# Query features of six tiles turned through memory instead of by TensorE

## The chip, the cores and the metric

The kernel runs on one core of one Trainium2 chip. The metric is the device time of one execution in microseconds (us). The engines are called PE (TensorE), DVE (VectorE), ACT (ScalarE), POOL (GpSimd) and SP (SyncE, which here only issues DMAs).

## The reference

Two branches work on one normalised input and are added to it:

```python
xn = layernorm(x)                                   # S=2048 rows, D=512
# branch A: linear attention, 32 heads of 16, features by two softmaxes
q, k, v = split(xn @ wqkv)
phi_q = concat(softmax(q @ w_phi), softmax(-q @ w_phi))
phi_k = concat(softmax(k @ w_phi), softmax(-k @ w_phi))
kv, z = phi_k^T v, sum(phi_k)
A = (phi_q kv / (phi_q z + 1e-6)) @ wo
# branch B: gated MLP with a product over the rows
z1, z2 = split(gelu(xn @ w_in)); z2 = layernorm(z2)
B = (z1 * (w_sp @ z2 + b_sp)) @ w_out
return x + A + B
```

## The kernel before

Rows are worked in 16 tiles of 128 (`NT`). Large products split each float operand into a rounded part and a remainder and do three matmuls (`mm3`, lines 56 to 58). Up to about 490 us the kernel computes the projections, the softmax features and the product with `w_sp`; what matters here is the last stage, which joins both branches.

At its start, the query features of tile `s` (unnormalised exponentials and reciprocal sums) lie in the DRAM tile `e_d`, and the gated values of branch B, already with features as rows, in `u_d`. The last stage walks over pairs of tiles `i`, `i + 1`. On PE a pair is:

1. `attend_T(i)`, called at the end of the pair before: the features of both tiles (128 rows by 1024 features each) are transposed into PSUM, 16 transposes of 128x128 (line 936, line 934 for the pair of tiles 2 and 3), and ACT copies them to four tiles `f` (features as rows, 256 columns). `f` has five buffers.
2. `project_u(i)`: 17 matmuls of `u` with `w_out` (`pout`).
3. `attend`: 16 small matmuls of the stationary `kvT` with `f` (`po`, line 951), which ACT and DVE split into `oT`.
4. `project_u(i + 1)`.
5. `project_o(i)` and `project_o(i + 1)`: 12 matmuls each of `oT` with `wo` into the same `pout`. ACT copies the sum out, and POOL adds it to `out` by an accumulating DMA.

Ahead of that run the preparations. `load_q` (line 535, SP) loads the features `et` of a tile from `e_d`, five tiles ahead. `features(s)` (three tiles ahead) calls `q_fin` (lines 542 to 549, DVE), which divides them by the attention's denominator in place, using a scratch tile `qtmp`; then a DMA issued by POOL (line 905) copies the result to a tile `er` of another number kind, of which there are six. `fetch_u` (lines 813 and 814, SP) loads `u` and its rest `rt` four tiles ahead; `gated` splits `u` into `uh` (ACT) and `ul` (DVE). The gated values of tiles 14 and 15 are made late, inside pair 8: DVE turns them in 32x32 blocks into `zt` (line 795, STREAM_TRANSPOSE), and SP stores them to `u_d` in four DMAs (line 798), with runs of 128 bytes.

`et` and `qtmp` share one pool of 16 slots (`slot`) with other tiles of this stage. The order on each engine is set by a planner that simulates the program while it is built: it takes what is ready, by the order of the program, and so lets preparations run ahead on an idle engine. `issue_after(ins)` keeps the instructions of its block behind `ins`, but only those on the engine of `ins`. The queues of the engines are then worked in that fixed order; an instruction that waits holds up what stands behind it on its engine, and this holds for the DMAs that SP issues.

Of the kernel before, what the change touches and what calls it, by code (L numbers as in the profile page):

```python
# [10 lines left out]
F32 = mybir.dt.float32  # L11
# [7 lines left out]
P = 128  # L19
# [4 lines left out]
NG = 4  # L24
NF = 2 * D
# [3 lines left out]
BL = 32  # L29
EPS_LN = 1e-5  # L30
EPS_DEN = 1e-6
XB = 5
FT, LT = 6, 13
NP = NT // 2
HP, QP = P // 2, P // 4
FP = 3 * P
# [4 lines left out]
def mixer(ctx: ExitStack, tc: tile.TileContext, x, x_t, wv, wqkT, phi_bd, wo, w_in, wst, b_r, w_out, out):  # L41
    nc = tc.nc
    pe, act, dve, pool, sp = nc.tensor, nc.scalar, nc.vector, nc.gpsimd, nc.sync
# [27 lines left out]
    def xz_tile(n, dt, name):  # L71
        return xz.tile([P, SL], dt, tag="xz", name=name)[:, :n]

    mid = ctx.enter_context(ExitStack())
    dram = ctx.enter_context(tc.tile_pool(name="dram", bufs=1, space=DRAM))
# [2 lines left out]
    u_d = dram.tile([NT, FU, P], F32, name="u_d")  # L78
    kvT_d = dram.tile([P, D], F32, name="kvT_d")
    zb_d = dram.tile([P, NF], F32, name="zb_d")  # L80
    nm_d = dram.tile([NT, ND, P], F32, name="nm_d")

    ident = cst.tile([P, P], F32, name="ident")
# [13 lines left out]
    def heads(ap):  # L97
        return ap.rearrange("p (h d) -> p h d", d=DH)

    def group(e, j):  # L100

        return e[:, j * P:(j + 1) * P]

    def pairs(ap, a):
        return ap.rearrange("p (h a) -> p h a", a=2)[:, :, a]

    def bc(ap, n):
        return ap.unsqueeze(2).to_broadcast([P, n, DH])
# [25 lines left out]
    def zproj(ps, s, w, order=(0, 1)):  # L134

        if ps in (za, kv_ps_p):
            p = [ps.tile([P, D], F32, tag="z", name="zps") for _ in range(2)]
        else:
            q = ps.tile([P, 2, D], F32, tag="z", name="zps")
            p = [q[:, k] for k in range(2)]  # L140
        t = xT[s]
        for k, j in enumerate(order):
            for c in range(ND):
                cs = slice(c * P, (c + 1) * P)
                zproj.last = mm3(p[k][:, :FC], (t[:, 0, cs], t[:, 1, cs]), (w[j][0][:, c], w[j][1][:, c]), c == 0, c == ND - 1)
        return [(slice(k, k + 1), p[k][:, :FC].unsqueeze(1)) for k in range(2)] if ps in (za, kv_ps_p) else [(slice(0, 2), q[:, :, :FC])]
# [28 lines left out]
    with ExitStack() as p0:  # L175
        res = p0.enter_context(left("p0res", 1))
        wk = p0.enter_context(left("p0wk", 2))
# [234 lines left out]
        t = xz_tile(2 * D, F32R, "xT").rearrange("p (a b) -> p a b", a=2)  # L412
# [18 lines left out]
        p = ps.tile([P, D], F32, tag="mm", name="proj")  # L431
# [7 lines left out]
        p = ps.tile([P, D], F32, tag="mm", name="proj")  # L439
# [18 lines left out]
        p = ps.tile([P, D], F32, tag="mm", name="proj")  # L458
# [79 lines left out]
    def q_fin(et, tmp, zb):  # L538

        e, r, t, w = et[:, :NF], *(et[:, NF + k * 2 * H:NF + (k + 1) * 2 * H] for k in range(3))  # L540
        den = et[:, NF + 6 * H:QW]
        dve.tensor_tensor(tmp, e, zb, op=ALU.mult)
        dve.tensor_reduce(t, heads(tmp), axis=AX.X, op=ALU.add)
        dve.tensor_tensor(t, t, r, op=ALU.mult)
        dve.scalar_tensor_tensor(den, pairs(t, 0), EPS_DEN, pairs(t, 1), op0=ALU.add, op1=ALU.add)
        dve.reciprocal(den, den)
        dve.tensor_tensor(w.rearrange("p (h a) -> p h a", a=2), r.rearrange("p (h a) -> p h a", a=2),
                          den.unsqueeze(2).to_broadcast([P, H, 2]), op=ALU.mult)
        return e, dve.tensor_tensor(heads(e), heads(e), bc(w, 2 * H), op=ALU.mult).ins

    QC = 4
    NQ = NT // QC
    NC = NP * NQ


    SEQ = [(i, q) for i in range(NP) for q in (range(NQ) if i < NP - 1 else (1, 2, 3, 0))]

# [5 lines left out]
    def load_a(n):  # L563
        i, q = SEQ[n]
        f = []
        for k in range(2):
            t = ws.tile([P, QC, P], F32, tag=f"f{k}", bufs=2, name="wf")
            sp.dma_start(t, wst[2 * i + k, :, q * QC:(q + 1) * QC, :])
            f.append(t.rearrange("p (k two) t -> p two k t", two=2))
        return f  # L570

    def prep_a(n, f):

        a, b = f
        pl = hl[n % 2]
        ops = {}

        def parts(names, src):
            t = pl.tile([P, 2, len(names), 2, P], F32R, tag="".join(names), name="A")
            prep_a.last = b_parts(t[:, 0], t[:, 1], src)  # L580
            for k, m in enumerate(names):
                ops[m] = t[:, 0, k], t[:, 1, k]

        sums = (sm[0].tile([P, 4, 2, P], F32, name="S") if sm else
                zw.tile([P, 4, FC], F32, tag=("T", "z2")[n], bufs=n + 1, name="S").rearrange("p a b -> p (a b)")[:, :8 * P].rearrange("p (a k b) -> p a k b", a=4, k=2))
        parts(("A11", "A12"), a)
        dve.tensor_tensor(sums[:, 0], b[:, 0], b[:, 1], op=ALU.add)
        dve.tensor_tensor(sums[:, 1], sums[:, 0], a[:, 0], op=ALU.subtract)  # L588
        parts(("S1", "S2"), sums[:, 0:2])
        dve.tensor_tensor(sums[:, 2], a[:, 0], b[:, 0], op=ALU.subtract)  # L590
        dve.tensor_tensor(sums[:, 3], a[:, 1], sums[:, 1], op=ALU.subtract)
        parts(("S3", "S4"), sums[:, 2:4])
        parts(("A22",), b[:, 1:2])
        return ops
# [3 lines left out]
    with ExitStack() as p1:  # L598
        tmp1 = p1.enter_context(left("tmp1", 1))
        kvT = tmp1.tile([P, D], F32, name="kvT")  # L600
        zb = tmp1.tile([P, NF], F32, name="zb")
# [41 lines left out]
        for s in range(NE):  # L643
            et = load_q(s, tb.tile([P, QW], F32, name="et") if s else tmp1.tile([P, 4, D], F32, tag="zhl", name="et").rearrange("p a b -> p (a b)")[:, :QW])
            tmp = zw.tile([P, 4, FC], F32, tag="z2", bufs=2, name="qtmp").rearrange("p a b -> p (a b)")[:, :NF]
            e, _ = q_fin(et, tmp, zb)
# [57 lines left out]
    for s in range(NT):  # L704
        p = zproj((kv_ps_p, zc, zbp, za)[s % 4], s, w2, (0, 1) if s % 2 == 0 else (1, 0))
# [7 lines left out]
        for k, q in p:  # L713
            ins = act.activation(z[:, k], q, AF.Gelu_apprx_tanh, scale=r_x[:, s:s + 1]).ins
# [35 lines left out]
    def load_z1(i):  # L750
        t = gt.tile([P, 2, FH + REM], F32, tag="z1", name="z1t")
        for k in range(2):
            pool.dma_start(t[:, k, :FH], z1_d[2 * i + k])  # L753
        return t

    def products(n, g):
        i, q = SEQ[n]
        ops = A.pop(n)
        for name, an, bn in FORM:
            if n % NQ == 0:  # L760
                g[name] = psg.tile([P, D], F32, tag="g", name="g")
            dst = g[name][:, :FC]
            for k in range(2):
                (ah, al), (bh, bl) = ops[an], B[2 * q + k][bn]
                mm3(dst, (ah[:, k], al[:, k]), (bh, bl), n % NQ == 0 and k == 0, n % NQ == NQ - 1 and k == 1)
# [16 lines left out]
    def gate(i, cb, z, u, ut, after=None):  # L782
# [10 lines left out]
        def turn():  # L793
# [3 lines left out]
            for b in range(0, P, BL):  # L797
                (pool if i == NP - 2 else sp).dma_start(dst[:, :, b:b + BL], src[b:b + BL].rearrange("p (m b) -> p m b", b=BL))

        return turn  # L800

    def slot(name, dt=F32):
        return xz_tile(2 * FH, dt, name)
# [44 lines left out]
    g, es, ets = {}, {}, {}  # L848
    for n in range(NC):
        i = SEQ[n][0]  # L850
        if n % NQ == 1 and i < NP - 1:
            z = load_z1(i)
        products(n, g)
        if n % NQ == NQ - 1 and i < NP - 1:
            c = gt.tile([P, 2, FU], F32, tag="c", name="c")
            cq = c[:, :, :FH].rearrange("p k (j f) -> p k j f", j=2)
            cb = drain(i, g, cq)
            g = {}
        if n + 3 < NC:
            raw[n + 3] = load_a(n + 3)  # L860
        if n + 2 < NC:
            A[n + 2] = prep_a(n + 2, raw.pop(n + 2))
        if n % NQ == NQ - 1 and i < NP - 1:
            turn = gate(i, cb, z, c, z, prep_a.last)
# [4 lines left out]
        if n == NC - 3:  # L869
            zs = slot("zb", F32R)  # L870
            zb, ident_r = zs[:, :NF].bitcast(F32), zs[:, NF:NF + P]
# [5 lines left out]
        if n == NC - 2:  # L877
            es[0], es[1] = first_q(0), first_q(1)
            t = xz_tile((KF + 1) * P, F32R, "u1")
# [10 lines left out]
    wk = ctx.enter_context(left("cwk", 2))  # L890
# [5 lines left out]

    def features(s):
        with tc.issue_after(fin[-1]):
            es[s], ins = q_fin(ets.pop(s), slot("qtmp")[:, :NF], zb)
        fin.append(ins)  # L900
        if s == 3:
            return
        e = es[s]
        es[s] = cw.tile([P, NF], F32R, tag="er", bufs=6, name="er")
        lasts[6] = pool.dma_start(es[s].bitcast(F32), e).ins
# [19 lines left out]
    def attend_T(s):  # L925

        fs = []
        for g in range(NG):
            pt = pst.tile([P, 2, 2, P], F32, tag="tr", name="ptq")
            for a in range(2):  # L930
                for k in range(2):
                    src = group(es[s + k], 2 * g + a)
                    if src.dtype == F32:
                        pe.transpose(pt[:, a, k], src, ident)
                    else:
                        pe.transpose(pt[:, a, k].bitcast(F32R), src, ident_r)  # L936
            f = wk.tile([P, 2, 2 * P], F32, tag="f", bufs=NG + 1, name="f")
            lasts[5] = act.activation(f, pt.rearrange("p a k b -> p a (k b)"), AF.Copy).ins
            fs.append(f)
        return fs  # L940
# [50 lines left out]
    GATE_LAST = 8  # L991

    fT = attend_T(0)
    wk.tile([P, D], F32, tag="xr", bufs=3, name="xr")
    wk.tile([P, 10 * QP], F32, tag="gap", name="gap")
# [20 lines left out]
    p, nxt = {}, dict(enumerate(uT))  # L1016
# [61 lines left out]
```

## Time and profile before

| | us |
|---|---|
| median of 3 runs | 625.21 (624.02 to 629.76) |
| the profiled execution | 625.34 |
| its span, first to last instruction | 623.6 |
| busy in the span: PE, DVE, ACT, POOL | 615.1, 508.3, 272.8, 113.7 |
| mean granted clock of PE | 0.999 |

Times in the rows of the profile count from the start of the span. A row of a timeline gives the start, the duration, the engine, the line and what it does; several alike in sequence are merged and counted with x. In brackets stands the idle time before it and what ended it. Matmuls overlap, so the distance between two starts says more than a duration.

### The profile page before, as it was taken

To read this page: it belongs to the slowest core of one execution; us is meant where nothing else is said; L and a number is where in the kernel's file an instruction comes from. 1 tells how busy PE (TensorE), PEld (TensorE's weight loads), DVE (VectorE), ACT (ScalarE), POOL (GpSimd) and SP (SyncE) were. 2 spreads that over 40 slices of the span, in tenths; PEclk is the share of its full clock that TensorE was granted. 3 is DMA by queue.
4 is the path that set the end of the run, shared out by engine and by line. 5 is a ranking of instruction groups with operands and counts; after the bars stand their busy time and mean duration, and the time that the engine had idled before them with its cause. 6 is when DMAs were issued, how large, how long until landed. Compare 5 with 4: busy or idle time off the path is not lost.

```text
span 623.6 us, 11439 instructions
## 1 busy us (share of the span) xinstructions
PE 615.1 (99%) x4366; PEld 561.5 (90%) x4366; DVE 508.3 (82%) x903; ACT 272.8 (44%) x436; POOL 113.7 (18%) x198
## 2 busy tenths in 40 slices
PE   8999999999999999999999999999999999999997
PEld 7888888878889999999999999999999887788785
DVE  5999899899988498988989888696959899989211
ACT  4652324333433558876435433253444433334331
POOL 4122233222211025541000000000000212211110
PEclk9999999999999999999999999999999999999999
DMA  9557676566546757002464745637477799984722
GB/s 318 189 138 165 162 183 187 152 165 172 118 154 186 271 210 270 2 1 67 129 128 136 196 89 155 156 97 173 88 177 244 225 284 332 328 243 111 162 38 48
DMA packets 90671, 103.67 MB, mean 166 GB/s; under 512 B 47080, under 2 KB 60136, under 8 KB 90376
## 3 DMA queue, kind: packets, MB, share of 16 engines
q1 hardware_dynamic: 76840, 60.76, 34.0%
q0 software_dynamic: 11472, 36.54, 23.6%
q10 hardware_dynamic: 2304, 5.64, 2.4%
q8 instruction: 34, 0.56, 0.4%
q14 instruction: 21, 0.17, 0.1%
HBM read 61.61 MB, written 30.56 MB: 148 GB/s over the span
## 4 chain that ended last, share of the span: by engine, by line
PE 85%; DMA 6%; DVE 4%; issue 3%; POOL 1%; ACT 1%; DVEq 0%; POOLq 0%
PE g L58 11%; PE g L57 10%; PE g L56 10%; PE zps L58 6%; PE zps L56 6%; PE zps L57 6%; PE pout L56 5%; PE pout L58 5%; PE pout L57 5%; DMA xc<-nm_d 5%; PE proj L56 4%; PE proj L57 4%; PE proj L58 4%; PE ptq L936 1%; PE po L951 1%
## 5 line engine op out<-in xcount | busy, mean ns | idle before, releaser
L57 PE MATMUL g<-B,A 128*128 128x344 f32 x448 | 143.4, 320 | 0.0
L56 PE MATMUL g<-B,A 128*128 128x344 f32 x448 | 142.9, 320 | 0.0
L58 PE MATMUL g<-B,A 128*128 128x344 f32 x448 | 140.7, 321 | 0.1
L56 PEld LDWEIGHTS g<-B,A 128*128 128x128 f32 x448 | 84.3, 188 | 0.0
L57 PEld LDWEIGHTS g<-B,A 128*128 128x128 f32 x448 | 84.2, 188 | 0.0
L58 PEld LDWEIGHTS g<-B,A 128*128 128x128 f32 x448 | 83.7, 188 | 0.4 <-DVE A L52 0.4
L48 ACT ACTIVATE A<-S 128x512 fp32r<-128x512 f32 x64 | 39.2, 629 | 76.3 <-DVE S L588 61.3
L121 ACT ACTIVATE e<-e,r_x 128x1024 f32<-128x1024 f32 x26 | 29.9, 1150 | 56.3 <-DVE e L120 55.1
L56 PE MATMUL proj<-wqk_h,xT 128*128 128x512 f32 x128 | 50.1, 391 | 0.0
L57 PE MATMUL proj<-wqk_l,xT 128*128 128x512 f32 x128 | 50.0, 390 | 0.0
L58 PE MATMUL proj<-wqk_h,xT 128*128 128x512 f32 x128 | 49.9, 390 | 0.0
L48 ACT ACTIVATE A<-wf 128x512 fp32r<-128x512 f32 (+1 forms) x64 | 33.1, 519 | 33.3 <-DMA wf<-in_wst 12.6
L52 DVE TENSOR_TENSOR A<-S,A 128x512 fp32r<-128x512 f32 x64 | 43.0, 686 | 4.4 <-ACT A L48 4.0
L56 PE MATMUL zps<-w_0h,xT 128*128 128x344 f32 x128 | 41.1, 321 | 0.0
L56 PE MATMUL zps<-w_1h,xT 128*128 128x344 f32 x128 | 40.9, 319 | 0.0
L58 PE MATMUL zps<-w_0h,xT 128*128 128x344 f32 x128 | 40.8, 319 | 0.0
L58 PE MATMUL zps<-w_1h,xT 128*128 128x344 f32 x128 | 40.7, 319 | 0.0
L57 PE MATMUL zps<-w_1l,xT 128*128 128x344 f32 x128 | 40.6, 318 | 0.0
L57 PE MATMUL zps<-w_0l,xT 128*128 128x344 f32 x128 | 40.6, 318 | 0.0
L753 POOL DMA_DIRECT2D z1t<-z_d x16 | 8.6, 545 | 166.9 <-DMA u_d<-z1t 124.9
L52 DVE TENSOR_TENSOR A<-wf,A 128x512 fp32r<-128x512 f32 (+1 forms) x64 | 35.0, 549 | 1.8 <-ACT A L48 1.8
L124 DVE TENSOR_REDUCE sm<-e 128x64 f32<-128x1024 f32 x26 | 31.2, 1200 | 1.7 <-ACT e L121 1.5
(218 smaller groups left out, 1430.6 us busy)
## 6 DMA issues: line engine op xcount, KB each, us to landing
wf<-in_wst SPq DMA_DIRECT2D x64, 256.0 KB, 3.1
e_d<-e POOLq DMA_DIRECT2D x16, 544.0 KB, 5.0
et<-e_d SPq DMA_DIRECT2D x16, 544.0 KB, 5.2
er<-et POOLq DMA_DIRECT2D x12, 512.0 KB, 5.5
z_d<-z1f ACTq DMA_DIRECT2D x16, 344.0 KB, 2.3
z1t<-z_d POOLq DMA_DIRECT2D x16, 344.0 KB, 5.3
zacc<-e POOLq DMA_DIRECT2D x10, 512.0 KB, 4.7
u<-u_d SPq DMA_DIRECT2D x15, 320.0 KB, 6.3
```

Of the source, the lines that this page charges most:

```text
L48: return act.activation(h, src, AF.Copy).ins
L52: return (eng or dve).tensor_tensor(l, src, h.bitcast(F32), op=ALU.subtract).ins
L56: pe.matmul(dst, ah, bh, start=start, stop=False)
L57: pe.matmul(dst, ah, bl, start=False, stop=False)
L58: return pe.matmul(dst, al, bh, start=False, stop=stop).ins
L121: softmax_pair.last = less, act.activation(e, e, AF.Exp, scale=scale).ins
L124: dve.tensor_reduce(sm, heads(e), axis=AX.X, op=ALU.add)
L753: pool.dma_start(t[:, k, :FH], z1_d[2 * i + k])
L936: pe.transpose(pt[:, a, k].bitcast(F32R), src, ident_r)
L951: lasts[3] = pe.matmul(po[r][c * QP:(c + 1) * QP, k], kvT[rows, m // 2, cols], fs[m // 4][rows, m // 2 % 2], start=True, stop=True).ins
```

## The change

For tiles 10 to 15 (`TQ = 10`), the features are not copied to `er`. DVE turns them in 32x32 blocks into `qtmp` (one instruction on 128x1024), and SP stores them in four DMAs to a new DRAM tile `q_d`, which holds the features of a pair as rows and its 256 positions as columns. Each DMA takes 32 partitions and writes runs of 32 floats, 128 bytes. `attend_T` of these three pairs then makes no transposes and no ACT copies: it loads each of the four `f` tiles (256 KB, rows of 1 KB) from `q_d` by SP. Pairs 0 to 8 stay as they are.

```diff
+TQ = 10
+    q_d = dram.tile([NP, NF, 2, P], F32, name="q_d")
+    def turn_q(s, dst, e):
+        ins = dve.transpose(dst, e).ins
+        q = q_d[s // 2, :, s % 2].rearrange("(m j) t -> j m t", j=BL)
+        for b in range(0, P, BL):
+            turn_q.last = sp.dma_start(q[:, :, b:b + BL], dst[b:b + BL].rearrange("p (m t) -> p m t", t=BL)).ins
+        return ins
+
+    def load_f(s, f, g):
+        sp.dma_start(f, q_d[s // 2, 2 * g * P:2 * (g + 1) * P].rearrange("(a p) k t -> p a (k t)", p=P))
+        return f
@@ def features(s):
         with tc.issue_after(fin[-1]):
-            es[s], ins = q_fin(ets.pop(s), slot("qtmp")[:, :NF], zb)
+            tmp = slot("qtmp")[:, :NF]
+            es[s], ins = q_fin(ets.pop(s), tmp, zb)
+            if s >= TQ:
+                ins = turn_q(s, tmp, es.pop(s))
         fin.append(ins)
+        if s >= TQ:
+            return
@@ def attend_T(s):
         fs = []
+        if s >= TQ:
+            return [load_f(s, wk.tile([P, 2, 2 * P], F32, tag="f", bufs=NG + 1, name="f"), g) for g in range(NG)]
```

## The prediction

> **What bounds the kernel now.** I read the page first, its busy times and the chain that ended last, then the last 127 us, where the edit lies, stage by stage, and then the timelines of the engines there.
>
> ```profile
> PE 615.1 (99%) x4366; PEld 561.5 (90%) x4366; DVE 508.3 (82%) x903; ACT 272.8 (44%) x436; POOL 113.7 (18%) x198
> ...
> PE 85%; DMA 6%; DVE 4%; issue 3%; POOL 1%; ACT 1%; DVEq 0%; POOLq 0%
> ```
> ```profile
> 497.00:540.00 43.00, 43.00 (x288) 34.37 (x272) 40.51 (x64) 15.18 (x27) 9.43 (x14) 1.00 1.03 314
> 540.00:580.00 40.00, 40.00 (x280) 31.56 (x280) 36.02 (x56) 16.51 (x29) 7.76 (x12) 1.00 0.73 195
> 580.00:610.00 30.00, 30.00 (x205) 23.82 (x205) 3.77 (x5) 10.23 (x19) 3.41 (x4) 1.00 0.48 96
> ```
>
> The columns of the stages are: length, then busy time of PE, weight loads, DVE, ACT and POOL, the granted clock, the DMA share and GB/s. PE is busy in every microsecond from 497 to 610 at full clock, and the chain is PE's. DVE is nearly full up to 580 (36.02 of 40) and almost empty after that. The DMA engines are full up to 540 and have room later. So what counts in the tail is PE's string of work; the other engines count only if they make it wait. In order of time, the chain shows that string for the pairs of tiles that the edit touches (10/11, 12/13, 14/15):
>
> ```profile
> 571.16 1.34 PE ptq L936 x16
> ...
> 576.46 1.02 PE po L951 x32
> 577.48 0.43 PE pout L56
> ...
> 587.07 1.31 PE ptq L936 x16
> ...
> 592.36 1.02 PE po L951 x32
> ...
> 602.97 1.34 PE ptq L936 x16
> ...
> 608.27 1.02 PE po L951 x32
> ```
>
> A pair costs 15.9 us (576.46 to 592.36): 16 transposes of query features (L936), the first tile's `w_out` product, the attention (`po`), the second tile's `w_out` product, two `wo` products. No wait of another engine stands between them. The attention comes about 5.3 us after the transposes began; that is the time in which ScalarE now copies `f` out of PSUM.
>
> **The change part by part.** *Removed from PE:* 16 transposes in each of three pairs.
>
> ```profile
> 570.76 0.39 PE L58 MATMUL pout<-woh,oT 128*128 128x512 f32 x1
> 571.00 1.50 PE L936 MATMUL ptq<-zb,er 128*128 128x128 f32 x16
> 572.33 0.46 PE L56 MATMUL pout<-wu,uh 128*128 128x512 f32 x1
> 572.63 0.39 PE L57 MATMUL pout<-wu,uh 128*128 128x512 f32 x1
> ```
>
> From the last `wo` matmul to the second `w_out` matmul there are 572.63 - 570.76 = 1.87 us. Without the transposes two pitches would be left; one pitch is 571.00 - 570.76 = 0.24 (0.23 elsewhere), so 0.46. That saves 1.41 us a pair. By the chain's own pieces it is 1.34, 1.31 and 1.34, so the sum lies between **3.99 and 3 x 1.41 = 4.23 us**. I take 4.2, since the slow first matmul after the transposes goes as well. Is something else late next? The first `w_out` product behind the freed place needs the split `u` of tile 10, and the second one the output buffer that ScalarE empties:
>
> ```profile
> 560.66 0.83 DVE L52 TENSOR_TENSOR ul<-u,uh 128x640 fp32r<-128x640 f32 x1 [1.83 <-ACT uh L48]
> ```
> ```profile
> 571.24 0.60 ACT L983 ACTIVATE xr<-pout 128x512 f32<-128x512 f32 x1 [1.04 <-PE pout L58]
> ```
>
> The split is done by 561.5, ten microseconds before 571.2, and the buffer is empty by 571.8 and used again at 577.5. So nothing is.
>
> The transposes have another price in the groups, that of each by itself:
>
> ```profile
> L936 PE MATMUL ptq<-zb,er 128*128 128x128 f32 x96 | 8.9, 247 | 0.0
> ```
>
> Each lasts 247 ns, but the 96 of six pairs fill 8.9 us, 93 ns each: they overlap, and their places in the row are what counts. The Trainium skill, in "TensorE: Matmul & The Clock Gate", Part 4: PE-mode transpose, measured about 275 ns for one inside a kernel; 48 of those would be an estimated 13.2 us where I take 4.2. The durations agree with it and the pitch does not.
>
> *Removed elsewhere:* 12 ScalarE copies of `f` (4 a pair) and six `er<-et` copies issued by POOL. ScalarE and POOL are idle most of this stretch (16.51 and 7.76 of 40), so this gives nothing by itself; it frees DMA time.
>
> *Added to DVE:* six transposes of 128x1024. The one of 128x1472 is the nearest row:
>
> ```profile
> 548.95 1.22 DVE L549 TENSOR_TENSOR et<-et 128x1024 f32<-128x1024 f32 x1
> ...
> 561.66 1.22 DVE L549 TENSOR_TENSOR et<-et 128x1024 f32<-128x1024 f32 x1
> ...
> 569.55 1.22 DVE L549 TENSOR_TENSOR et<-et 128x1024 f32<-128x1024 f32 x1
> ...
> 571.82 1.71 DVE L795 STREAM_TRANSPOSE zt<-z1t 128x1472 f32<-128x1472 f32 x1
> ...
> 577.32 1.22 DVE L549 TENSOR_TENSOR et<-et 128x1024 f32<-128x1024 f32 x1
> 578.45 1.28 DVE L52 TENSOR_TENSOR oT<-po,oT 128x512 fp32r<-128x512 f32 x2
> ```
> ```profile
> 581.42 0.40 PE L56 MATMUL pout<-woh,oT 128*128 128x512 f32 x1
> ```
>
> 1.71 x 1024/1472 = 1.19 us each, 7.1 us in all (at most 6 x 1.71 = 10.3). The L549 rows end the features of tiles 11, 13, 14 and 15 (550.2, 562.9, 570.8, 578.5). DVE has 4.0 us idle between 540 and 580, so the last features come some 3 us later (between 2 with all idle time used and 6 with none). That lies beside PE: before, tile 15's features were ready 25 us ahead of their use at 603. What PE does wait for on DVE are the `oT` remainders, queued among the features: here they end at 579.7, and the `wo` products begin at 581.42. A transpose put ahead of them costs at most 1.2 us, inside that 1.7. I price it at 0; with the cover gone it is 1.2 a pair.
>
> *Added to SP:* 24 stores of 128 KB in pieces of 128 bytes, and 12 loads of 256 KB.
>
> ```profile
> 552.54 0.55 SPq L535 DMA_DIRECT2D et<-e_d  x1
> 573.55 5.84 SPq L798 DMA_DIRECT2D u_d<-zt  x4
> 584.66 0.38 SPq L813 DMA_DIRECT2D u<-u_d  x1
> ...
> 586.17 0.47 SPq L814 DMA_DIRECT2D rt<-u_d  x1
> ```
> ```profile
> SPq L798 <- DVE zt L795: 20.4, 1, 20.4
> ...
> SPq L813 <- DMA u_d<-zt: 5.1, 2, 3.4
> ```
> ```profile
> q1 hardware_dynamic: 7488, 1.51, 26.5%
> ...
> wf<-in_wst SPq DMA_DIRECT2D x64, 256.0 KB, 3.1
> ...
> u<-u_d SPq DMA_DIRECT2D x15, 320.0 KB, 6.3
> ...
> u_d<-zt SPq DMA_DIRECT2D x4, 184.0 KB, 4.6
> ```
>
> The stores of `zt` are of the same kind: four in 5.84 us of SP. By size, a tile's four take 5.84 x 128/184 = 4.1 us of SP and land 4.6 us later. The queue row is from the DMA view of 570 to 600: 26.5% of 16 engines over 30 us is 127 engine-us for 7488 packets, 17 ns each. So a tile's 4096 pieces occupy all 16 engines for 4.4 us, 26 us in all six, and the share of 0.73 and 0.48 in the two stages leaves 10.8 + 15.6 = 26 us; the loads of `f` take the place of the six `er` copies, which move the same bytes. It fits, without anything to spare. The Trainium skill ("DMA: Bandwidth & Descriptors", Specifications) sets 512 bytes as the least size for the full rate, which speaks against this store. The trace agrees: 128 bytes in 17 ns on 16 engines is 120 GB/s, where the full stretch moved 314.
>
> A load is priced at 0.4 us of SP, landing after 3.1 (`wf`) to 6.3 us (`u`); I take the upper, as the DMA engines are busy.
>
> *Added waits.* The stores wait for DVE's transpose; behind them in SP's order stand the loads of later tiles and the `zt` stores. SP issued nothing from 553 to 573.5, so this is free. The loads of `f` wait for the stores and for the attention of the pair before, which holds four of the five `f` buffers; behind them stand tile 14's and 15's `u`, the last `x` and the last stores. The attention waits for `f`; behind it stands all of PE. `qtmp` is held until the stores land, about 10 us, but the last `et` load was issued at 552.5 for features that end at 578.5 and take about 6 us, so a late slot has cover.
>
> When is `f` due? At 576.46 - 1.41 = 575.0, 592.36 - 2.82 = 589.5 and 608.27 - 4.23 = 604.0. When is it there?
> - Pair 10: features 11 end at about 552 with a transpose of lag, turned by 553, stored by 557 and landed by 562; buffers are free at 561.5. Loads issued by 564 land by 570: 5 us early.
> - Pair 12: buffers are free at 577.48 - 1.41 = 576.1; features 13 landed by 576. If the loads go out then, they land by 584. If they stand behind tile 14's stores and `zt`'s (575 to 579, then to 584.4), they are issued by 586 and land between 589.1 and 592.3: a wait of 0 to 2.8 us.
> - Pair 14: features 15 are turned by 582.7, stored by 587, landed by 591.4; buffers are free at 590.6. Loads land by 600: 4 us early.
>
> **Sum:** 625.34 us for the profiled execution (span 623.6) less 4.2 is 621.1. The median shown is 625.21, which is the same within 0.02%, so **621.1** stands for both.
>
> **The rivals.**
> 1. *Pair 12's loads stand behind the `zt` stores.* For it: both become ready at about 576 on one queue. Against it: the loads may go first, and the shorter landing just fits. Late DVE remainders end in the same place. Price 1 to 4 us in all: 622 to 625, say 623.2.
> 2. *Slower: pair 12's loads stand behind the `u` loads of tiles 14 and 15.* Those wait on SP until the `zt` stores have landed (the 5.1 us in SP's waits). With the lag that is 584.4 + 4.6 = 589.0; the `u` and `rt` loads take to 590.9, `f` is issued by 592.5 and lands between 595.6 and 598.8. PE waits 6 to 9 us and gives back more than it got: 621.1 + 6 to 9 = **627 to 630**, say 628. It decides from the point where `f` lands more than 4.2 us after 589.5. Against it: the `u` loads become ready 8 us later than the `f` loads. Over 1% slower needs a wait of 10.5 us.
> 3. *Each transpose is worth its whole duration to PE:* 48 x 0.247 = 11.9 us, so 613.5. The two pitches around 16 of them, 1.87 us, speak plainly against it. The Trainium skill's 275 ns stands for this case.
> 4. *The change doesn't do what it says:* PE finds another wait in the freed place and the time stays at 625. The two rows on the split `u` and the output buffer speak against it.
>
> **How the numbers follow.** Forecast (no notable wait) 0.57; rival 1 0.22; rival 2 0.12; rival 3 0.02; rival 4 0.07. One per cent, 6.3 us, is about what a measurement here can tell from no change. All but rival 3 and the far end of rival 2 lie within it: faster 0.05 (rival 3, and some for an order of the queues that helps elsewhere), slower 0.05, same 0.90. The range takes in the forecast with its size between 3.99 and 4.23 and the spread of the runs (the lowest, 624.02, is 1.2 under the median, so 619.8 and a little), rival 1, and rival 4 with 1 us of spread above 625.2: **619.5 to 626.2**.
>
> **What would show it.** Right: three stretches of 14.5 us between the attentions instead of 15.9, no `ptq` group ahead of the last three pairs, each attention directly behind its `w_out` product, DVE's last feature near 582, six STREAM_TRANSPOSE of 1.2 us. Wrong: weight loads of `po` that wait for a DMA of `f`, above all near 590, or `oT` remainders ending after their `wo` product should begin.

## The result, and the profile after

| | before | after |
|---|---|---|
| median of 10 runs, us | 625.93 (624.02 to 629.76) | 630.81 (627.46 to 632.72) |
| the profiled execution, us | 625.34 (span 623.6) | 632.72 (span 631.0) |
| ratio | 1 | 1.0073 [1.0051, 1.0096] |

The changed kernel is 0.7% slower. The prediction said 621.1 with a range up to 626.2. The profiled run of after is the slowest of its ten, 1.9 us above the median, so its account is a little longer than that of a typical run.

The chain that ended last, of after (start, duration, what):

```profile
576.38 1.09 PE po L972 x32
...
588.75 7.90 DMA u<-u_d
...
600.23 1.61 SPq L558
601.88 3.09 DMA q_d<-qtmp
605.04 0.38 SPq L562
605.47 6.84 DMA f<-q_d
612.36 2.47 PE po L972 x24
```

Before, this stretch of the chain was PE alone. Now it goes through a load of `u`, the stores of the turned features (L558), and the load of `f` for the last pair (L562). The chain's link from that load of `u` to the stores is a DVE instruction on another tile (`oT`), so this link is doubtful. PE's side is in its timeline of after:

```profile
590.85 1.32 PE L972 MATMUL po<-f,kvT 64*32 64x256 f32 x16
593.22 1.31 PE L972 MATMUL po<-f,kvT 64*32 64x256 f32 x16 [1.06 <-DMA f<-q_d]
594.46 0.50 PE L57 MATMUL pout<-wu,uh 128*128 128x512 f32 x1
...
610.40 0.64 PE L972 MATMUL po<-f,kvT 64*32 64x256 f32 x8 [2.42 <-DMA f<-q_d]
612.36 2.47 PE L972 MATMUL po<-f,kvT 64*32 64x256 f32 x24 [1.32 <-DMA f<-q_d]
614.76 0.79 PE L57 MATMUL pout<-wu,uh 128*128 128x512 f32 x1
615.35 0.63 PE L58 MATMUL pout<-wu,uh 128*128 128x512 f32 x1
615.78 0.63 PE L59 MATMUL pout<-wu,ul 128*128 128x512 f32 x1
```

In this timeline pair 10's attention starts at 576.31 without a wait and pair 12's at 590.85, 14.54 us later, where before it was 15.90: the gain of 1.4 us a pair is there. Then the `f` tiles come late, and PE takes 594.46 - 590.85 = 3.61 us for pair 12's attention, where before it took 1.02. Pair 14's `f` tiles come later still. The 7.4 us between the two spans are made up like this:

| us | |
|---|---|
| +1.4 | already there at pair 4 (530.10 against 528.73), ahead of all changed work |
| -4.2 | the transposes of three pairs (1.44, 1.36, 1.43) |
| +2.6 | wait of pair 12's attention for `f` |
| +5.8 | wait of pair 14's attention: due at 607.9, next product at 614.76, so 6.84 instead of 1.02 |
| +1.6 | the product after it at a lower clock: 5.15 instead of 3.53 |
| +0.2 | rest |

The first row is scatter between runs: in the kernels below, the same point lay between 527.7 and 532.1.

The clock is seen in the windows of after (length, PE, weight loads, DVE, ACT, POOL, granted clock, DMA share, GB/s):

```profile
546.00:613.00 67.00, 62.12 (x393) 47.04 (x392) 43.54 (x61) 17.51 (x29) 6.87 (x8) 0.99 0.93 190
608.00:612.00 4.00, 0.64 (x8) 0.18 (x8) 0.00 (x0) 0.00 (x0) 0.00 (x0) 0.92 0.99 277
612.00:616.00 4.00, 3.64 (x27) 1.64 (x28) 0.49 (x1) 1.09 (x2) 0.00 (x0) 0.50 0.18 68
```

And the same 67 us of before:

```profile
546.00:613.00 67.00, 67.00 (x441) 53.38 (x440) 35.49 (x55) 24.25 (x42) 9.65 (x13) 1.00 0.55 131
```

The DMA engines were 55% busy there and are now 93% busy, which leaves 5 us of room in 67. DVE has 8 us more to do and PE 5 us of holes. The queue that carries the new traffic is SP's, in its timeline of after:

```profile
555.85 6.13 SPq L558 DMA_DIRECT2D q_d<-qtmp  x4
565.58 0.38 SPq L562 DMA_DIRECT2D f<-q_d  x1
...
573.50 6.58 SPq L558 DMA_DIRECT2D q_d<-qtmp  x4
580.18 4.41 SPq L812 DMA_DIRECT2D u_d<-zt  x4
584.82 3.21 SPq L562 DMA_DIRECT2D f<-q_d  x4
588.13 0.45 SPq L558 DMA_DIRECT2D q_d<-qtmp  x1
588.75 1.03 SPq L827 DMA_DIRECT2D u<-u_d  x1
589.83 3.15 SPq L828 DMA_DIRECT2D rt<-u_d  x1
593.02 3.63 SPq L558 DMA_DIRECT2D q_d<-qtmp  x3
596.75 1.79 SPq L827 DMA_DIRECT2D u<-u_d  x1
...
599.21 3.33 SPq L558 DMA_DIRECT2D q_d<-qtmp  x4
605.04 1.99 SPq L562 DMA_DIRECT2D f<-q_d  x4
```
```profile
SPq L562 <- DMA q_d<-qtmp: 5.8, 4, 3.5
```

The second fence is from the waits of SP: the loads of `f` waited 5.8 us for stores to land, four times. The longest of these waits, 3.5 us, is the gap in the first fence: from 562.0 to 565.6 SP stood still for the landing of tile 11's stores, with the DMA engines only 65% busy, while tile 12, turned by 561.9, waited behind it until 567.0. Between 573 and 605 of before, SP issued two batches and was otherwise idle. Now tile 13's stores hold it until 580.1, the `zt` stores until 584.6, pair 12's loads until 588.0, tile 14's stores until 596.7, tile 15's until 602.5. One DMA issue takes anything from 0.3 us to 4.2 us of SP:

```profile
L558 SPq DMA_DIRECT2D q_d<-qtmp x24: 313/627/4207, 548.1 to 601.9; - x24
```

(The row of the tile `q_d`: shortest, median and longest duration in ns.) The features were ready long before their stores went out, as DVE's timeline of after shows for tiles 14 and 15:

```profile
580.22 1.23 DVE L555 STREAM_TRANSPOSE qtmp<-et 128x1024 f32<-128x1024 f32 x1
586.86 1.25 DVE L555 STREAM_TRANSPOSE qtmp<-et 128x1024 f32<-128x1024 f32 x1
```

Tile 15 was turned at 588.1, its stores started at 599.2 and had landed by 605.0, and only then did the loads of `f` go out.

### The profile page after: what moved, and what is told of

Its sections match the earlier page's. It is cut to its first block, busy times and chain, and to the rows that moved or that the text cites. A ratio compares the mean times of both kernels' runs of the same rounds, so it can differ in the third digit from the quotient of the medians.

```text
span 631.0 us, 11364 instructions
## 1 busy us (share of the span) xinstructions
PE 616.8 (98%) x4318; PEld 558.8 (89%) x4318; DVE 515.6 (82%) x909; ACT 267.2 (42%) x424; POOL 110.5 (18%) x192
## 4 chain that ended last, share of the span: by engine, by line
PE 79%; DMA 10%; DVE 5%; issue 2%; SPq 2%; POOL 1%; ACT 0%; POOLq 0%; DVEq 0%; ACTq 0%
PE g L59 10%; PE g L58 10%; PE g L57 10%; PE proj L57 6%; PE proj L58 6%; PE proj L59 6%; PE zps L59 5%; PE zps L57 5%; PE zps L58 5%; PE pout L57 3%; PE pout L58 3%; PE pout L59 3%; DMA et<-e_d 2%; DMA xc<-nm_d 2%; DMA u<-u_d 1%
## 5 line engine op out<-in xcount | busy, mean ns | idle before, releaser
L123 ACT ACTIVATE e<-e,r_x 128x1024 f32<-128x1024 f32 x26 | 29.9, 1150 | 56.3 <-DVE e L122 55.1
```

What stands on the lines that cost most here:

```text
L123: softmax_pair.last = less, act.activation(e, e, AF.Exp, scale=scale).ins
```

## The experiments

Theories as they stood: **the DMA engines' time** (the stores of 128-byte pieces fill them, and everything in the queue comes late), against **the order on SP** (loads of `f` stand behind stores, `u` loads and their waits, which a different issuing engine would cure), **DVE's transposes**, and **the place of pair 12** alone. The shares of occupancy below are the DMA share of 546 to 613 less the 0.60 of the first experiment, which has no stores of features, times 67 us. Ratios are to the kernel before, run on the same chip.

**No turn and no stores (e1).** The loads of `f` read the same number of bytes straight from `e_d`, with unturned features.

```diff
-                ins = turn_q(s, tmp, es.pop(s))
+                es.pop(s)
-        sp.dma_start(f, q_d[s // 2, ...])
+        sp.dma_start(f, e_d[s:s + 2, :, 2 * g * P:2 * (g + 1) * P].rearrange("a p n -> p a n"))
```

> Left out: the DVE transposes and the 24 stores; the f tiles of pairs 10, 12 and 14 are loaded by SP from e_d instead, with the same bytes and run length (so the values of these tiles are other ones). PE's transposes and ScalarE's copies are gone as in the changed kernel. Theory A (what costs is the stores: their time on SP and on the DMA engines): the loads go out when their buffers come free, PE never waits, the full 4.2 us appear: 621 to 622.5 against 625.9 before. Rival B (the loads of 1 MB a pair are late by themselves, or taking the transposes off PE gives less than their places): 624 or more, with po waiting for f.

621.66 us, ratio 0.993 [0.9906, 0.9953]. The chain of e1:

```profile
560.29 1.02 PE po L972 x32
574.76 1.02 PE po L972 x32
589.23 1.02 PE po L972 x32
603.71 1.02 PE po L972 x32
```
```profile
546.00:613.00 67.00, 67.00 (x418) 53.09 (x417) 35.91 (x56) 18.75 (x31) 6.87 (x8) 1.00 0.60 133
```

Three distances of 14.47 us and (second fence, its windows) no hole in PE. The gain on PE is what the prediction's first term says, and the loads cost nothing. The loss is in the turn, the stores, or the order.

**The same bytes in long runs (e2).** DVE turns, and the stores write 4 KB runs; the values reach the attention in another order.

```diff
-        q = q_d[s // 2, :, s % 2].rearrange("(m j) t -> j m t", j=BL)
+        q = q_d[s // 2].rearrange("f k t -> (f k t)")[s % 2 * P * NF:(s % 2 + 1) * P * NF].rearrange("(p n) -> p n", n=NF)
-            turn_q.last = sp.dma_start(q[:, :, b:b + BL], dst[b:b + BL].rearrange("p (m t) -> p m t", t=BL)).ins
+            turn_q.last = sp.dma_start(q[b:b + BL], dst[b:b + BL]).ins
```

> Only the shape of the stores is changed: each of the four DMAs of a tile writes 32 runs of 4 KB in place of 1024 runs of 128 bytes (the bytes and the order on SP are nearly the same; the values are stored in another order, so those of tiles 10 to 15 are other ones). Theory A1 (the 128-byte pieces fill the DMA engines and through them hold SP): a tile's stores take 1.5 us of SP instead of 4 to 6.6, f of pair 14 lands before 604, the time falls to 621.5 to 623.5. Rival A2 (the order on SP, with its waits for landings, is what makes f late, whatever the pieces): a wait of 2 us or more stays before the attention of pair 14, 625 to 629.

621.64 us, ratio 0.9927 [0.99, 0.9954]: the whole gain. SP's timeline and the windows of e2:

```profile
545.79 2.12 SPq L558 DMA_DIRECT2D q_d<-qtmp  x4
553.50 1.72 SPq L558 DMA_DIRECT2D q_d<-qtmp  x4
```
```profile
546.00:613.00 67.00, 67.00 (x421) 53.23 (x420) 43.80 (x63) 18.16 (x29) 7.31 (x9) 1.00 0.76 187
```

DVE has the same work as in after (43.80 against 43.54) and PE has no hole, so DVE's transposes are not the cause. The stores take SP about 2 us a tile where after's take 3.3 to 6.6, and the DMA engines (0.76 - 0.60) x 67 = 11 us in all, where after's take 22.

**The long runs twice (e5).** To tell the DMA engines' time from the pieces themselves, each 4 KB store was made twice, to two places.

```diff
-            turn_q.last = sp.dma_start(q[b:b + BL], dst[b:b + BL]).ins
+            for d in (q2_d, q_d):
+                q = d[s // 2].rearrange(...)[...].rearrange("(p n) -> p n", n=NF)
+                turn_q.last = sp.dma_start(q[b:b + BL], dst[b:b + BL]).ins
```

(The diff is against e2.)

> As the kernel with 4 KB runs, but each store is made twice, the first time to a second DRAM tile that nobody reads (48 stores; values of tiles 10 to 15 are in another order). By the DMA shares from 546 to 613 a tile's stores took 3.6 us of all engines in runs of 128 bytes and 1.7 in runs of 4 KB, so twice 1.7 is the occupancy of the small runs with large ones. Theory A1 (what makes f late is the engines' occupancy, and SP held by it): waits before pair 12 or 14 come back, 625 to 631. Rival A3 (small runs are late by something else than occupancy, such as the landing of many small writes): still no wait, 621 to 623.

628.16 us, ratio 1.0028 [1.0001, 1.0054]. PE's timeline and the windows of e5:

```profile
593.33 0.64 PE L974 MATMUL po<-f,kvT 64*32 64x256 f32 x8 [1.17 <-DMA f<-q_d]
...
611.15 0.64 PE L974 MATMUL po<-f,kvT 64*32 64x256 f32 x8 [1.43 <-DMA f<-q_d]
```
```profile
546.00:613.00 67.00, 62.65 (x400) 47.63 (x383) 43.58 (x62) 18.48 (x30) 6.88 (x8) 1.00 0.90 236
```

At (0.90 - 0.60) x 67 = 20 us of occupancy, the waits of both pairs are back, without any short piece. It has twice as many issues on SP, too; but e2 and after have the same number, and differ by the whole loss.

**Without pair 12 (e7), and pair 10 alone (e8).** Tiles 12 and 13 go the old way in e7 (`TQ = (10, 11, 14, 15)`, `if s in TQ`); tiles 12 to 15 in e8 (`if TQ <= s < 12`).

> Tiles 12 and 13 go the old way (er, transposes on PE); tiles 10, 11, 14 and 15 as in the changed kernel, with runs of 128 bytes. 2.8 us of PE's work are gone. Theory A1 (the stores of six tiles, zt's and the loads fill the stretch from 548 to 607): with a third less the last f lands in time, 623 to 624.5. Rival A4 (tile 15's store stands behind the u loads, which wait for zt's landing, whatever else is stored): pair 14 still waits 2 to 5 us, 626 to 630.

> Only tiles 10 and 11 take the new way. All theories: no wait, 1.4 us gained, 624.5 to 625.3; if a store costs PE or the others something even where nothing is late, 626 or more.

623.78 us, ratio 0.9952 [0.9929, 0.9975], and 624.51 us, ratio 0.9967 [0.9945, 0.9988]. The windows of e7:

```profile
546.00:613.00 67.00, 67.00 (x423) 53.14 (x423) 42.11 (x61) 20.48 (x34) 7.94 (x10) 1.00 0.82 173
```
With two pairs turned the engines are 82% busy and PE has no hole (nor has it in e8). The medians are 2.4 and 1.7 us below the kernel before, 1.4 a pair within their intervals. In e7 pair 14 is turned by the same stores as in after and has no wait, so nothing is wrong with pair 14's place; it is what the third pair adds, its stores and its loads on SP together, that makes it late. This run alone does not tell the two apart.

**The stores issued by POOL (e3), the loads issued by POOL (e4).** One word each: `sp.dma_start` becomes `pool.dma_start`, in e3 for the stores in `turn_q`, in e4 for the loads in `load_f`.

> The 24 stores of 128-byte pieces are issued by POOL instead of SP; all else as in the changed kernel. Theory A2 (SP's one queue is the bottleneck): SP is free, each store goes out when its tile is turned, f of pair 14 lands 8 us earlier, 621.5 to 624. Rival A1 (the pieces fill the DMA engines): the engines are as full as before, f of pairs 12 and 14 is still late, 627 to 631.

> The 12 loads of f are issued by POOL instead of SP, so SP no longer stands still for the landing of stores; the stores stay on SP. Theory A2: the waits for landings on SP (5.8 us in all) go, tile 12's store goes out 4 us earlier, but tile 15's still stands behind the u loads: 625 to 628. Rival A1: SP's time goes into pieces, not into those waits: 629 to 631, as the changed kernel.

e3: 634.78 us, ratio 1.0125 [1.0092, 1.0159], the slowest of all and above both expected ranges. PE's timeline, the windows and the DMA issues (KB each, us to landing) of e3:

```profile
599.34 3.75 PE L972 MATMUL po<-f,kvT 64*32 64x256 f32 x32 [9.66 <-DMA f<-q_d]
```
```profile
592.00:596.00 4.00, 0.00 (x0) 0.00 (x0) 0.00 (x0) 0.00 (x0) 0.00 (x0) 0.84 1.06 233
596.00:600.00 4.00, 0.66 (x8) 0.22 (x8) 0.00 (x0) 0.00 (x0) 0.00 (x0) 0.50 0.97 285
```
```profile
q_d<-qtmp POOLq DMA_DIRECT2D x24, 128.0 KB, 6.6
...
u_d<-zt SPq DMA_DIRECT2D x4, 184.0 KB, 12.4
```

Taking the stores off SP did not help: they land after 6.6 us instead of 4.5, the `zt` stores after 12.4 instead of 4.8 (after's medians), and pair 12 waits 9.66 us with the engines at a share of 1.06. The traffic is only moved to another place. Against after, e3 is slower by 4.0 us in the medians, but the two intervals of the ratio just meet (1.0092 and 1.0096).

e4: 627.21 us, ratio 0.9999 [0.9976, 1.0022], so 3.6 us of the loss are recovered in the medians; the intervals of e4 and after lie apart. Its windows:

```profile
546.00:613.00 67.00, 64.63 (x421) 49.21 (x420) 44.94 (x64) 19.28 (x31) 15.80 (x20) 1.00 0.92 189
```

The engines are as full as in after (0.92), but PE loses 2.4 us of the 67 instead of 4.9, and the clock does not fall. This points to SP's order as a part of the cause: where `f` loads wait on SP for stores to land, the stores behind them wait too, as tile 12's did from 562.0 to 565.6 in after.

**The `u` loads of tiles 14 and 15 issued by POOL (e9).** This takes away what the prediction's slower rival named.

```diff
+        eng = pool if i >= NT - 2 else sp
-        sp.dma_start(u, u_d[i, :KF * P].rearrange("(k p) t -> p k t", p=P))
+        eng.dma_start(u, u_d[i, :KF * P].rearrange("(k p) t -> p k t", p=P))
```

(The same for `rt`.)

> As the changed kernel (runs of 128 bytes), but u and rt of tiles 14 and 15 are loaded by POOL, so that on SP the stores of tiles 14 and 15 no longer stand behind loads that wait for zt's landing. If the order on SP makes up most of pair 14's wait, its stores are out by 597 and f lands by 604: 623 to 625.5. If the engines' occupancy alone does it, f of pair 14 is as late as before: 629 to 631.

629.8 us, ratio 1.0046 [1.0023, 1.0068]. SP's and PE's timelines of e9:

```profile
589.13 12.85 SPq L558 DMA_DIRECT2D q_d<-qtmp  x8
604.83 2.05 SPq L562 DMA_DIRECT2D f<-q_d  x4
```
```profile
610.57 3.19 PE L973 MATMUL po<-f,kvT 64*32 64x256 f32 x32 [2.93 <-DMA f<-q_d]
```

No load stands between the eight stores of tiles 14 and 15 now, and they still take until 601.98, against 602.54 in after, and `f` is issued at 604.83 against 605.04. (This execution reached pair 4 1.3 us later than after's, so against its own start the stores are out 1.9 us earlier.) They take 6.4 us a tile, and from 589 to 602 the DMA share is 0.97 to 1.10, so the engines are full. The waits of SP put 2.6 us of the 12.85 down to a DVE instruction on `oT`; tile 15 had been turned by 589.4, so it is doubtful that the stores waited for that. Pair 14's attention still loses 5.1 us here (5.8 in after). So the `u` loads and their waits were not what held most of it, though the chain of after passes through one of them. A small part they may be: the medians differ by 1.0 us, with overlapping intervals.

**Runs of 256 bytes (e6), with the `u` loads by POOL (e11), and with the `f` loads by POOL (e10).** The two tiles of a pair are written side by side by the last multiply of the features, so that DVE turns two halves of [128, 1024] per pair and a run in memory holds both tiles' 32 floats. The attention reads `f` with the columns put back in order by its operand's pattern.

```diff
-    q_d = dram.tile([NP, NF, 2, P], F32, name="q_d")
+    q_d = dram.tile([NP, NF, P // BL, 2 * BL], F32, name="q_d")
...
+        for n in range(2):
+            t = dst if n else slot("qt")[:, :NF]
+            ins = dve.transpose(t, e[n]).ins
+            q = q_d[s // 2, n * NF // 2:(n + 1) * NF // 2].rearrange("(m j) b t -> j m b t", j=BL)
+            for b in range(P // BL):
+                turn_q.last = sp.dma_start(q[:, :, b], t[b * BL:(b + 1) * BL].rearrange("p (m t) -> p m t", t=2 * BL)).ins
...
+        return f.rearrange("p (b k t) -> p k b t", k=2, t=BL) if i >= TQ else f
```

> The features of both tiles of a pair are laid side by side before DVE turns them, so that the stores write runs of 256 bytes: half as many packets for the same bytes; the columns of f then stand in another order, which the attention's moving operand undoes. A pair's stores go out together after its second tile. If a packet has a price of its own (17 ns here), a tile's stores take some 2 us of the engines and f is in time: 621 to 623.5. If bytes have the price, or if storing the first tile later makes f late: 626 to 631.

> The kernel with runs of 256 bytes, with u and rt of tiles 14 and 15 loaded by POOL. If the order on SP is what is left of the wait, 621 to 622.5; if the engines' occupancy is, 622.5 to 623.5, as without it.

> The kernel with runs of 256 bytes, with its 12 loads of f issued by POOL. It still waited 2 us for f in all; with SP free of the loads and their waits the stores of the last pair go out earlier: 621 to 622.5. If POOL's loads land later than SP's, 623 to 625.

e6: 622.96 us, ratio 0.9926 [0.9899, 0.9953]; e11: 622.94, ratio 0.9928 [0.9902, 0.9954]; e10: **622.41 us, ratio 0.9922 [0.9893, 0.9951]**, the lowest median of the kernels here that keep all the work and the place of each value, though the intervals of the three overlap. PE's timeline of e6, its windows, and those of e10:

```profile
593.36 0.64 PE L988 MATMUL po<-f,kvT 64*32 64x256 f32 x8 [0.75 <-DMA f<-q_d]
```
```profile
546.00:613.00 67.00, 66.25 (x433) 51.24 (x432) 45.68 (x71) 19.24 (x31) 6.87 (x8) 1.00 0.87 193
```
```profile
546.00:613.00 67.00, 67.00 (x426) 52.50 (x411) 43.85 (x68) 18.38 (x30) 15.89 (x20) 1.00 0.84 189
```

A wait of 0.75 us is left in e6 and none in e10. The occupancy came down only to (0.87 - 0.60) x 67 = 18 us in e6, where half the packets should have meant about 11 (in e10, with the same stores, it is 16 us): a packet of 256 bytes takes 18 x 16 / 12288 = 23 ns, one of 128 bytes 22 x 16 / 24576 = 14 ns. So the size of the runs alone is not the whole of e6's gain. Its stores also go out once a pair instead of once a tile, in another order. How much is the 4 us of occupancy and how much that order was not told apart; e11, within 0.02 us of e6, shows no part of the `u` loads in it.

## Why the prediction was wrong

**What held.** PE's string of work is the bound, and a pair without its transposes is 14.47 us long instead of 15.9 (predicted 14.5). The pitch was the right price, not the 247 ns of each transpose (the third rival). The transposes on DVE last 1.23 to 1.25 us (predicted 1.19) and delay nothing that PE needs (e2). The occupancy of the stores, sized at 17 ns a packet and 26 us in all, measured 14 ns and 22 us. The 17 ns were the mean of a row in which 2 x (640 + 96) = 1472 of the 7488 packets were the 512-byte rows of the two `u` and `rt` loads, so they were not the price of a 128-byte packet alone.

**The step that failed** is "When is it there?": it let the stores of tile 15 start the moment the tile was turned, and took SP as free for the stores ("SP issued nothing from 553 to 573.5, so this is free"). The part before it ends with "It fits, without anything to spare", and even that counted the room up to 610. For `f` to be there at 604, with the 6.3 us of a load, the last store had to be landed by about 598, and up to there the shares of before (0.73 from 540 to 580, 0.52 from 580 to 598) leave 10.8 + 8.6 = 19 us, less than the 26 us wanted or the 22 us measured. What did not fit stood in SP's queue. By the prediction, tile 15 was turned at 582.7, stored by 587 and landed by 591.4; it was turned at 588.1, its stores started at 599.2, 11.1 us later, went out by 602.5 and landed at 605.0. Pair 14's `f` was to come at 600, 4 us early; it came at 612.4, 4.5 us after it was due. In those 11.1 us SP was issuing tile 14's stores and the `u` and `rt` loads; tile 14's stores had themselves stood behind tile 13's, the `zt` stores and pair 12's loads of `f`. The length of a single store was not what was missing: the 4.1 us of SP came from `zt` stores that met full engines (a share of 1.01 from 573.5 to 579.4), and the six tiles' stores took 29.9 us, 5.0 each, tile 15's 3.3.

Two smaller terms in the same step pointed the same way. The lag of DVE was taken as 3 us, "between 2 with all idle time used and 6 with none"; tile 15's features ended 6.9 us later than before, the 1.4 us of drift not counted, more than either end. And what a wait costs was taken as its length: after 5.8 us of late `f`, PE ran the next product at a granted clock of 0.50, 1.6 us more.

**The rivals.** The first (pair 12's loads behind the `zt` stores, 1 to 4 us) is what pair 12 did: loads issued at 584.8 to 588.0, where the prediction has 586, and 2.6 us lost. It was given as an alternative to the forecast, but came together with a larger wait that no case had, that of pair 14. The second rival had the sign and nearly the size (627 to 630), for another reason: pair 12's loads went out ahead of the `u` loads of tiles 14 and 15 (584.8 against 588.8), not behind them, and most of the loss is pair 14's, which e9 does not take away. That its number came near is luck. That the change does nothing (625) does not hold; it gains and loses.

**What stays open.** e4 shows that with equally full engines (0.92 and 0.93) another issuer of the loads recovers 3.6 us, and e3 that another issuer of the stores can also be worse; which of the waits on SP carries that was not tried one by one, and how the loss divides between the engines' time and the order on SP is not measured. The part of e6's gain that is order is open, as said above.

## What to carry to other kernels

Price a stream of small transfers twice: once as occupancy of the DMA engines over the whole stretch in which it must fit, and once as a queue, each piece starting when the one before it is done. Count the room only up to the time when the last piece is needed. If the first sum says "no room to spare", the second must let every piece stand behind those ahead of it, and the last piece is the one to check, since here the backlog was largest there. Longer runs, or fewer tiles turned this way (two pairs of three kept their gain), helped in every run here, where another issuing engine helped in one place and hurt in another; and one wait of several microseconds on PE costs its clock as well.

## What the runs showed of the hardware

- The granted clock fell to 0.50 after PE had been nearly idle for 4 us (0.64 us of work between 608 and 612 in after), and within the wait of 9.66 us in e3. The pitch was then 0.43 us instead of 0.23. In e9 one gap of 2.93 us before the small matmuls of `po` was enough (0.50 from 612 to 614). Four waits of 0.67 to 1.43 us in e5, two and two with short work between, left it at 1.00. The Trainium skill ("TensorE: Matmul & The Clock Gate", Why this matters for your kernels) advises no gaps above about 3 us between bursts of matmuls. The fall in e3 agrees with it; in e9 (2.93 us) and in after (2.42 and 1.32 us with 0.64 us of work between them) no single gap was above 3 us and the clock fell all the same.
- The issue of one store on SP lasted 0.31 to 4.2 us in after, where the DMA engines were 93% busy, 0.31 to 0.83 us with runs of 4 KB (e2, 76%), and 0.30 to 2.3 us with those made twice (e5, 90%). It thereby holds up everything behind it. Before, the four `zt` stores, 5.84 us, showed it, and single loads of `u` and `rt` of up to 1.8 us from 497 to 503; the engines were full in both stretches (1.01 and 1.04).
- Packets of 4 KB took 11 x 16 / 768 = 0.23 us of an engine, of 256 bytes 23 ns (21 by e10), of 128 bytes 14 ns. From 128 to 256 bytes a packet takes about 1.6 times as long, so doubling the run saved a fifth to a quarter of the time for the same bytes, not half.
- Another issuing engine changed more than the time of the issue: the same 24 stores issued by POOL (e3) landed after 6.6 us instead of 4.5, the four `zt` stores of SP after 12.4 us instead of 4.8, and the kernel was 4.0 us slower than after; the 12 loads issued by POOL (e4) made it 3.6 us faster than after. The order and the times at which the transfers start change with the engine, so these runs do not show which of them did it.
